# A fused attention, gate and tanh product kernel: fixed steps for each part of a weight conversion, half stores, a third memory for weight pairs, and loads of the last weights one at a time

## The chip, the cores and the metric

The kernel runs on one core of a Trainium2 chip. The metric is the device time of one execution in microseconds (us). The engines are TensorE (PE: matmuls; PEld is its weight load), VectorE (DVE), ScalarE (ACT), GpSimd (POOL) and SyncE (SP). In this kernel every DMA is issued by SP, in the order of the program. Each engine works through its own instructions in order and waits only where an operand or a buffer is not ready.

## The reference

Causal attention with a decay bias gives x (2304 tokens by 512), then a gated product, then a tanh product:

```python
x = attention(q, k, v, s)                                   # 2304 x 512
h1 = 1 / (1 + exp(-(x @ w_gate))) * (x @ w_val)             # 2304 x 1536
y = h1 @ w_out                                              # 2304 x 512
h = y @ w_in                                                # 2304 x 2048
out = (h - tanh(h)) @ w_out2                                # 2304 x 512
```

The weights arrive as 64-bit words and become float32 on the chip.

## The kernel before

**Number format.** Matmuls are done on float32 values split in two: a high part (h), which TensorE's fp32r format holds, and the rest (l). A product is three matmuls: h by h, l by h and h by l. ScalarE makes a high part by a copy; VectorE or GpSimd makes the low part by a subtraction.

**Strassen (Winograd form).** The two products with w_in and w_out2 are done on 2 by 2 blocks with seven products instead of eight. Each operand becomes seven blocks, some of them sums of others. A *weight pair* p (0 to 7) takes rows or columns p and p + 8 of a weight matrix and gives a tile of [128, 2, 7, 256]: high and low parts of seven blocks. *Left* pairs belong to w_in (used in the tanh product), *right* pairs to w_out2 (used in the last product).

**Stages.** Attention and the gate come first (lines 610 to 844) and are not touched. Then:

- *The out-projection loop* (lines 909 to 931): 72 steps, six token blocks of 384 by 12 slices m of 128. A step loads a slice g four steps ahead (`gload`, line 818), splits one two steps ahead into gh (ScalarE, line 826) and gl (VectorE, line 827), with three buffers each and five for g, and issues 12 matmuls (lines 918 to 922). After a block's last slice, `ydrain` takes the four accumulators out, and `ysingle` or `ysums` makes sums (`ydiff`, line 880, VectorE) and splits (`ysplit`, ScalarE line 876, GpSimd line 877), all at once. Beside this, the loop converts the eight right pairs and two left pairs.
- *The tanh product* (lines 963 to 1123): 24 groups (p, j), eight pairs by three double blocks of tokens. A group has seven products of six matmuls (line 991) in the order 1, 6, 7, 2, 5, 4, 3, each drained by ScalarE or VectorE (lines 994 to 1012), then tanh and a subtraction, and two stores of h. Between products `between` runs a step of the six further left conversions, a chore for the last y, or a load of a half right pair.
- *The last product* (lines 1178 to 1196): five token stretches by eight pairs, 40 steps of up to 42 matmuls of 256 columns, and `sprep`, which makes the left operand s from h read back.

**A conversion** (class `PairConversion`, lines 143 to 234) is a list of 14 actions per pair: two scalings of raw words (`words_scale`, ScalarE, line 82), two joins (`words_join`, VectorE, lines 86 and 87), the loads of the next pair, the store of the last pair, four additions (GpSimd, line 184), and high and low parts in two cuts (ScalarE line 199; GpSimd for the first and VectorE for the second, line 204). `tick` runs the next action; the loop calls it so often that the ten conversions end with the 72 steps. Right pairs are made in one tile `stage` and stored to memory (line 855) with a single DMA. Left pairs go to two tiles, `wo0` and `wo1`, in turn. The first two groups of the tanh product write to a tile `temp`, whose tag `wd` holds right pair 0 from the third group on.

Of the kernel before, what the change touches and what calls it, by code (L numbers as in the profile page):

```python
# [67 lines left out]
def attention_moe_moe2(ctx: ExitStack, tc: tile.TileContext, kqT, v, s, wg, wv, wo, win, wo2, out):  # L68
# [15 lines left out]
    def words_join(tmp, raw):  # L84
        lo = raw.bitcast(U).rearrange("p (n two) -> p n two", two=2)[:, :, 0]
        DVE.tensor_scalar(out=tmp, in0=tmp, scalar1=3, scalar2=None, op0=ALU.logical_shift_left)
        DVE.scalar_tensor_tensor(out=tmp, in0=lo, scalar=29, in1=tmp,  # L87
                                 op0=ALU.logical_shift_right, op1=ALU.bitwise_or)

# [53 lines left out]
    class PairConversion:  # L143


        def __init__(self, work, jobs, dst, rest):
            self.raws = [work[:, 0:1024], work[:, 1024:2048]]
            self.u = work[:, 2048:4096].rearrange("p (n c) -> p n c", c=256)
            self.jobs, self.dst, self.rest = jobs, dst, rest
            self.step, self.kept = 0, None  # L150
            self.steps = [f for p in range(len(jobs)) for f in self.pair(p)]
            self.marks = []
            self.load(0)

        def load(self, p):
            if p < len(self.jobs):
                for s in range(2):
                    SP.dma_start(out=self.raws[s], in_=self.jobs[p][1][s])

        def keep(self):  # L160
            if self.kept:
                self.kept()
                self.kept = None

        def pair(self, p):
            kind, _, m = self.jobs[p]
            left = kind == "left"
            t = {"u": self.u, "f": self.u.bitcast(F)}

            def spot(s):  # L170
                return t["u"][:, 2 - 2 * s:4 - 2 * s].rearrange("p a c -> p (a c)")

            def start():
                words_scale(spot(0), self.raws[0])

            def second():
                words_scale(spot(1), self.raws[1])

            def join(s):
                return lambda: words_join(spot(s), self.raws[s])  # L180

            def add(o, x, y, op):
                def f():
                    POOL.tensor_tensor(out=t["f"][:, o], in0=t["f"][:, x], in1=t["f"][:, y], op=op)  # L184
                return f

            if left:
                todo = ((4, 0, 1, ALU.add), (6, 2, 0, ALU.subtract), (5, 4, 2, ALU.subtract), (7, 3, 5, ALU.subtract))
                cuts = ((0, 3, 1), (3, 7, 1))
            else:  # L190
                todo = ((4, 3, 2, ALU.subtract), (6, 1, 3, ALU.subtract), (5, 1, 4, ALU.subtract),
                        (7, 0, 5, ALU.subtract))
                cuts = ((0, 3, 0), (3, 7, 1))

            def high(c0, c1, o):
                def f():
                    if "h" not in t:
                        t["h"], t["l"], t["store"] = self.dst(kind, m)
                    ACT.activation(out=t["h"][:, c0:c1], in_=t["f"][:, c0 + o:c1 + o], func=AF.Copy)
                return f  # L200

            def low(c0, c1, o, last):
                def f():
                    self.rest[last].tensor_tensor(out=t["l"][:, c0:c1], in0=t["f"][:, c0 + o:c1 + o],  # L204
                                            in1=t["h"][:, c0:c1].bitcast(F), op=ALU.subtract)
                    if last:
                        self.kept = t["store"]
                        self.marks.append(p)
                return f

            yield start
            yield second
            yield join(0)
            yield join(1)
            yield lambda: self.load(p + 1)
            yield self.keep
            for a in todo[:2]:
                yield add(*a)
            yield high(*cuts[0])
            for a in todo[2:]:  # L220
                yield add(*a)
            yield low(*cuts[0], False)
            yield high(*cuts[1])
            yield low(*cuts[1], True)
            yield lambda: None

        def tick(self):
            if self.step < len(self.steps):
                self.step += 1
                self.steps[self.step - 1]()  # L230

        def finish(self, p):
            while self.step < len(self.steps) and p not in self.marks:
                self.tick()
# [616 lines left out]
    def dst(kind, p):  # L851
        if kind == "left":
            w = slot[p] = wop.tile([128, 2, 7, 256], R, tag=f"wo{p % 2}", name=f"win{p % 2}")
            return w[:, 0], w[:, 1], None
        return stage[:, 0], stage[:, 1], lambda: SP.dma_start(out=w2scr[p], in_=stage.bitcast(F))

    lefts = [("left", [win[m].bitcast(U).rearrange("p k c -> p (k c)") for m in (p, p + MP)], p) for p in range(MP)]
    rights = [("right", [wo2[m * 128:(m + 1) * 128].bitcast(U) for m in (p, p + MP)], p) for p in range(MP)]
    cvt = PairConversion(work, rights + lefts[:2], dst, (POOL, DVE))
    per = len(cvt.steps) // len(cvt.jobs)  # L860

    ends = [(0, 0), (len(order) - 8, per * MP + 8), (len(order) - 4, per * (MP + 1) + 8),
            (len(order), per * (MP + 2))]

    def ticks(i):
        for (i0, s0), (i1, s1) in zip(ends, ends[1:]):
            if i < i1:
                return s0 + (i + 1 - i0) * (s1 - s0) // (i1 - i0)
# [40 lines left out]
    for i, (blk, m) in enumerate(order):  # L909
# [22 lines left out]
    cvt.finish(len(cvt.jobs) - 1)  # L932
    cvt.keep()
# [4 lines left out]
    cvt = PairConversion(work2, lefts[2:], dst, (POOL, DVE))  # L938
# [3 lines left out]
    temp = wd.tile([128, 3584], F, tag="wd", name="temp")  # L942
    yopen(NJ - 1)
    chores = ysingle(NJ - 1) + ysums(NJ - 1)
# [14 lines left out]

    HT = [fp.tile([128, BLK], F, name=f"ha{k}") for k in range(2)]  # L960
    he = {}

    def group(i, p, j, between):
        w, y = slot[p], Y_[j]
        if i < 2:
            ha, hc = HT
            hb = temp[:, 8 * BLK:9 * BLK]
            o = [temp[:, 2 * BLK * (2 * i + a):2 * BLK * (2 * i + a + 1)].rearrange("p (t c) -> p t c", t=2)
                 for a in range(2)]
        else:  # L970
            if i == 2:
                he["t"] = w2.tile([128, 2, BLK], F, tag="re", name="he")
                WO[0] = wd.tile([128, 2, 7, 256], R, tag="wd", name="wo2f")
                SP.dma_start(out=WO[0].bitcast(F), in_=w2scr[0])
# [9 lines left out]
        for n in PORD:  # L984
# [68 lines left out]
    def sprep():  # L1053
# [7 lines left out]
        if i < 2:  # L1061
            DP["s", i] = wop.tile([128, 2, 7, TB], R, tag=f"wo{i}", name="s")
        sh, sl = (DP["s", i % 2][:, x, :, 0:tb] for x in range(2))
# [3 lines left out]
        POOL.tensor_tensor(out=t[:, 1], in0=t[:, 0], in1=a11, op=ALU.subtract)  # L1067
        ACT.activation(out=sh[:, 0:3], in_=g[:, 1:4], func=AF.Copy)
        DVE.tensor_tensor(out=t[:, 3], in0=a12, in1=t[:, 1], op=ALU.subtract)
        DVE.tensor_tensor(out=sl[:, 0:3], in0=g[:, 1:4], in1=sh[:, 0:3].bitcast(F), op=ALU.subtract)  # L1070
        ACT.activation(out=sh[:, 3:7], in_=t, func=AF.Copy)
        DVE.tensor_tensor(out=sl[:, 3:7], in0=t, in1=sh[:, 3:7].bitcast(F), op=ALU.subtract)
# [3 lines left out]

    loads = []

    def wload(j):
        w = w2.tile([128, 3, 2, 7, 256], R, tag=f"y{j}", name=f"wo2{j}")  # L1080
        for x in range(3):
            WO[1 + 3 * j + x] = w[:, x]
            for q in range(2):
                loads.append((w[:, x, q], w2scr[1 + 3 * j + x][:, q]))

    def wfetch():
        if loads:
            out_, in_ = loads.pop(0)
            SP.dma_start(out=out_.bitcast(F), in_=in_)
# [150 lines left out]
```

## Time and profile before

| | us |
|---|---|
| runs (3), median | 1101.29 |
| lowest and highest | 1099.75, 1102.79 |
| profiled execution | 1103.57 |
| its span, first to last instruction | 1101.8 |

| engine | busy us | share of the span | instructions |
|---|---|---|---|
| PE | 1029.6 | 93% | 7070 |
| PEld | 1007.7 | 91% | 7070 |
| DVE | 728.9 | 66% | 1546 |
| ACT | 536.7 | 49% | 1191 |
| POOL | 539.2 | 49% | 663 |

Successive matmuls overlap in the record, so TensorE's busy share says little of its pace; the distance between starts does. The mean granted TensorE clock is 0.971 of full speed (2.4 GHz). An idle time is named in the rows by what ended it: `<-ACT gh L826` is the gh written by ScalarE on line 826. A wait for several things is put down to the one that came last.

### The profile page before, as it was taken

What the parts mean: (1) busy time and instruction counts of PE and PEld (TensorE: products, weight loads), DVE (VectorE), ACT (ScalarE), POOL (GpSimd) and SP (SyncE); (2) the same over time, 40 slices, a digit from 0 to 9 for tenths busy, and PEclk for the clock granted to TensorE, in tenths of its full rate; (3) what the DMA queues carried; (4) which work ended last, traced back from release to release, by engine and by line L of the source; (5) the groups of instructions that cost most, each with busy time, mean ns of one, the idle gap of its engine ahead of it and who ended that gap; (6) DMA issues with size and microseconds to landing.
All of it is one profiled execution on the core that took longest, in us unless ns stands there. A gap on an engine that the chain in (4) does not pass through costs nothing. (4 is left out here: it accounts for less than half of the span.)

```text
span 1101.8 us, 20467 instructions
## 1 busy us (share of the span) xinstructions
PE 1029.6 (93%) x7070; PEld 1007.7 (91%) x7070; DVE 728.9 (66%) x1546; ACT 536.7 (49%) x1191; POOL 539.2 (49%) x663
## 2 busy tenths in 40 slices
PE   8999999999999999999885867989999989999998
PEld 6899999999999999998785867889999989999998
DVE  7774567776666666374465655577877765888786
ACT  5774656766565665353433333454444433434342
POOL 3575456666565665143325425275555423355342
PEclk9999999999999999999887988899999999999999
DMA  8963457665566563175554575415444299444442
GB/s 214 260 207 107 128 154 195 184 176 169 166 162 173 163 170 94 67 240 178 178 182 144 175 245 184 172 68 220 154 162 153 105 354 358 141 124 139 130 138 74
DMA packets 107455, 187.50 MB, mean 170 GB/s; under 512 B 16276, under 2 KB 76440, under 8 KB 106072
## 3 DMA queue, kind: packets, MB, share of 16 engines
q1 hardware_dynamic: 107352, 186.20, 54.2%
q8 instruction: 55, 0.90, 0.3%
q14 instruction: 48, 0.39, 0.1%
HBM read 133.64 MB, written 52.50 MB: 169 GB/s over the span
## 5 line engine op out<-in xcount | busy, mean ns | idle before, releaser
L918 PE MATMUL bank<-gh,wo 128*128 128x384 f32 x288 | 106.5, 370 | 43.5 <-ACT gh L826 43.5
L991 PE MATMUL bank<-y,win 128*128 128x384 f32 x672 | 120.7, 340 | 4.2 <-ACT ha L994 3.7
L991 PEld LDWEIGHTS bank<-y,win 128*128 128x128 f32 x672 | 118.1, 190 | 5.8 <-ACT ha L994 5.8
L827 DVE TENSOR_TENSOR gl<-g,gh 128x384 fp32r<-128x384 f32 x72 | 58.3, 835 | 97.9 <-ACT gh L826 87.6
L1193 PE MATMUL bank<-wo,s 128*128 128x256 f32 x378 | 106.4, 281 | 2.2 <-DVE s L1070 2.1
L1191 PE MATMUL bank<-wo,s 128*128 128x256 f32 x378 | 105.9, 280 | 0.0
L1192 PE MATMUL bank<-wo,s 128*128 128x256 f32 x378 | 105.9, 280 | 0.0
L919 PE MATMUL bank<-gh,wo 128*128 128x384 f32 x288 | 104.5, 363 | 0.0
L918 PEld LDWEIGHTS bank<-gh,wo 128*128 128x128 f32 x288 | 60.8, 211 | 47.2 <-ACT gh L826 47.2
L500 DVE TENSOR_TENSOR ptl<-bank,pth 128x384 fp32r<-128x384 f32 (+1 forms) x92 | 49.8, 542 | 71.1 <-ACT pth L499 50.5
L499 ACT ACTIVATE pth<-bank 128x384 fp32r<-128x384 f32 (+1 forms) x92 | 44.1, 479 | 107.1 <-PE bank L475 88.8
L958 POOL TENSOR_TENSOR h<-he,h 128x384 f32<-128x384 f32 x44 | 47.5, 1093 | 87.4 <-ACT h L957 87.4
L184 POOL TENSOR_TENSOR work<-work 128x256 f32<-128x256 f32 x64 | 56.8, 898 | 65.6 <-DVE work L87 58.1
L1065 POOL TENSOR_TENSOR dg<-dg 128x256 f32<-128x256 f32 (+1 forms) x40 | 36.6, 915 | 89.3 <-DMA dg<-h 65.1
L604 DVE SCALAR_TENSOR_TENSOR th<-th,bank 128x256 f32<-128x256 f32 (+1 forms) x96 | 42.8, 447 | 47.8 <-PE bank L592 38.2
L1193 PEld LDWEIGHTS bank<-wo,s 128*128 128x128 f32 x378 | 71.2, 188 | 2.9 <-DVE s L1070 2.8
L1191 PEld LDWEIGHTS bank<-wo,s 128*128 128x128 f32 x378 | 71.2, 188 | 0.0
L344 POOL TENSOR_TENSOR kl<-kq,kh 128x576 fp32r<-128x576 f32 (+1 forms) x46 | 56.2, 1221 | 30.7 <-ACT kh L343 29.6
L1192 PEld LDWEIGHTS bank<-wo,s 128*128 128x128 f32 x378 | 71.2, 188 | 0.0
L475 PE MATMUL bank<-ident,sp 128*128 128x128 f32 x400 | 67.7, 274 | 1.6 <-ACT p L487 0.5
L922 PE MATMUL bank<-gl,wo 128*128 128x384 f32 x288 | 67.2, 358 | 0.7 <-DVE gl L827 0.7
L443 ACT ACTIVATE sp<-sp,nm 128x384 f32<-128x384 f32 (+3 forms) x108 | 67.3, 623 | 0.9 <-DVE nm L433 0.8
(381 smaller groups left out, 3395.3 us busy)
## 6 DMA issues: line engine op xcount, KB each, us to landing
h<-h SPq DMA_DIRECT2D x44, 384.0 KB, 3.6
kq<-in_kq SPq DMA_DIRECT2D x32, 448.0 KB, 3.5
w<-stage SPq DMA_DIRECT2D x8, 1792.0 KB, 9.2
g<-g SPq DMA_DIRECT2D x72, 192.0 KB, 5.9
wo<-w SPq DMA_DIRECT2D x12, 896.0 KB, 12.4
dg<-h SPq DMA_DIRECT2D x72, 128.0 KB, 2.3
cbc<-cum SPq DMA_DIRECT2D x32, 256.0 KB, 5.4
work<-in_wo SPq DMA_DIRECT2D x16, 512.0 KB, 3.7
```

The lines of the kernel that those rows point to most:

```text
L184: POOL.tensor_tensor(out=t["f"][:, o], in0=t["f"][:, x], in1=t["f"][:, y], op=op)
L344: POOL.tensor_tensor(out=kl, in0=d["k"], in1=kh.bitcast(F), op=ALU.subtract)
L443: ACT.activation(out=e["sp"], in_=e["sp"], func=AF.Exp, scale=-1.0, bias=e["m"], accum_out=e["sum"])
L475: PE.transpose(e["tr"][j // 4][:, j % 4, :], e["sp"][:, c:c + 128], ident)
L827: DVE.tensor_tensor(out=gl, in0=raw, in1=gh.bitcast(F), op=ALU.subtract)
L918: PE.matmul(acc[d], won[m][0][:, c], gh, start=(m == 0), stop=False)
L919: PE.matmul(acc[d], won[m][1][:, c], gh, start=False, stop=False)
L922: PE.matmul(acc[d], won[m][0][:, c], gl, start=False, stop=(m == M1 - 1))
L991: PE.matmul(ps, l, y[r][:, PR[n], k], start=(k + x == 0 and n != 2), stop=(k == 1 and x == 2), skip_group_check=(n == 2))
L1191: PE.matmul(o, sh[:, g, c], w[:, 0, f], start=(p == 0 and t == 0), stop=False)
L1192: PE.matmul(o, sh[:, g, c], w[:, 1, f], start=False, stop=False)
L1193: PE.matmul(o, sl[:, g, c], w[:, 0, f], start=False, stop=(p == MP - 1 and t == nt - 1))
```

## The change

- `PairConversion` and its `tick` are replaced by `PairWords`, whose parts can be called one by one, and `Plan`, a table from a step's number to the calls to be made in it. `words_join` is cut into a shift and an or.
- In the loop, right pair p has its scalings in step i = 7p + 3, its joins in i + 1 and i + 2, the additions in i + 3 and i + 4, high 0 in i + 4, low 0 in i + 5, high 1 in i + 6, low 1 in i + 7. Its loads are issued in i - 4 and i - 3; its store is two DMAs, high half in i + 8 and low half in i + 9. The two left pairs follow, the second in a work tile of its own.
- The chores of `ysums` and `ysingle` after a block are done one per step.
- Left pairs go to three tiles in turn, `wo0`, `wo1` and `wd`; `temp` serves the first four groups, with `ha` in turn. The conversions and the chores of the last y stand at fixed products in the tanh product. The last tanh and subtraction of a group are put behind the first drain of the next (`hend`).
- Right pairs 0 to 5 are loaded in halves into the y tiles when these come free, one half every 3.5 products; pairs 6 and 7 in halves in the first four steps of the last product. The order of groups is changed (`seq`), and `sprep` for the first two steps is made in six pieces (`sparts`) at fixed products of the last groups.

```diff
-    class PairConversion:
...
+    class PairWords:
...
+        def load(self, s):
+            SP.dma_start(out=self.raws[s], in_=self.jobs[s])
...
+        def high(self, k):
+            c0, c1, o = self.cuts[k]
+            if self.to is None:
+                self.to = self.dst()
+            ACT.activation(out=self.to[:, 0, c0:c1], in_=self.f[:, c0 + o:c1 + o], func=AF.Copy)
+
+        def low(self, k):
+            c0, c1, o = self.cuts[k]
+            (DVE if k else POOL).tensor_tensor(out=self.to[:, 1, c0:c1], in0=self.f[:, c0 + o:c1 + o],
+                                               in1=self.to[:, 0, c0:c1].bitcast(F), op=ALU.subtract)
+
+    class Plan:
+        def __init__(self):
+            self.at = {}
+
+        def put(self, i, f, *args):
+            self.at.setdefault(i, []).append((f, args))
+
+        def do(self, i):
+            for f, args in self.at.pop(i, []):
+                f(*args)
...
+    def left(p, w):
+        def dst():
+            slot[p] = (wd if p % 3 == 2 else wop).tile([128, 2, 7, 256], R, tag=("wo0", "wo1", "wd")[p % 3], name=f"win{p % 3}")
+            return slot[p]
+        return PairWords(w, True, [win[m].bitcast(U).rearrange("p k c -> p (k c)") for m in (p, p + MP)], dst)
+
+    def keep(p, q):
+        SP.dma_start(out=w2scr[p][:, q], in_=stage[:, q].bitcast(F))
...
+    for p in range(MP):
+        c = right(p)
+        i = 7 * p + 3
+        lay(c, {"load0": max(i - 4, 0), "load1": i - 3, "scale0": i, "scale1": i, "shift0": i + 1, "join0": i + 1, "shift1": i + 2, "join1": i + 2,
+                "add0": i + 3, "add1": i + 3, "add2": i + 4, "add3": i + 4, "high0": i + 4, "low0": i + 5,
+                "high1": i + 6, "low1": i + 7})
+        for q in range(2):
+            plan.put(i + 8 + q, keep, p, q)
...
-        while cvt.step < ticks(i):
-            cvt.tick()
+        plan.do(i)
+        if chores:
+            chores.pop(0)()
...
-                for f in (ysums if t else ysingle)(j):
-                    f()
+                chores.extend((ysums if t else ysingle)(j))
...
+    def hend():
+        if "end" in he:
+            he.pop("end")()
...
             if n == 1:
                 ACT.activation(out=ha, in_=ps, func=AF.Copy)
+                hend()
...
-                hfin(o[0][:, 1], ha, DVE)
-                store(0)
-            between()
+                he["end"] = lambda: (hfin(o[0][:, 1], ha, DVE), store(0))
+            plan.do(len(PORD) * i + len(P) - 1)
...
-    seq = [(0, 0), (0, 1), (1, 0), (0, 2), (1, 1), (1, 2)]
-    seq += [(p, j) for p in range(2, MP - 2) for j in range(NJ)]
-    seq += [(p, j) for j in range(NJ) for p in (MP - 2, MP - 1)]
+    seq = [(0, 0), (0, 1), (1, 0), (1, 1), (0, 2), (1, 2)]
+    seq += [(p, j) for p in range(2, MP - 3) for j in range(NJ)]
+    seq += [(p, j) for j in range(NJ) for p in range(MP - 3, MP)]
...
+    for k, f in zip((1, 2, 3, 5, 7, 8, 9, 10, 14, 15, 16), ysingle(NJ - 1) + ysums(NJ - 1)):
+        plan.put(k, f)
+    for p in range(2, MP):
+        k = n * (2 * p - 1 + (p == MP - 1))
+        h = (k + 13, k + 17) if p == 2 else (k + 7, k + 14)
...
+    for j in range(2):
+        k = n * (seq.index((MP - 1, j)) + 1)
+        plan.put(k, wload, j)
+        for x in range(6):
+            plan.put(k + 7 * x // 2, wfetch)
...
+    k = n * seq.index((MP - 1, NJ - 1))
+    for x, i in enumerate((k - 13, k - 11, k - 7, k - 6, k - 5, k - 3)):
+        plan.put(i, next, parts[0], None)
+        plan.put(i + n, next, parts[1], None)
...
     for i, (s, p) in enumerate(dsteps):
+        if loads:
+            wfetch()
```

## Rows read from the trace of the kernel before

**Rows 1.** Busy time by stage: stretch, length, busy (instructions) by engine, granted clock, DMA.

```profile
505.05:721.28 216.23, 172.03 (x867) 168.01 (x865) 113.98 (x141) 77.75 (x135) 83.50 (x64) 0.87 0.53 181
721.28:914.85 193.57, 181.77 (x1010) 178.89 (x1009) 143.77 (x231) 82.09 (x154) 97.93 (x86) 0.97 0.51 186
914.85:1096.90 182.05, 179.89 (x1513) 179.02 (x1512) 143.13 (x191) 69.32 (x85) 76.92 (x79) 1.00 0.49 149
```

**Rows 2.** TensorE's timeline at the loop's start: start, length, instruction.

```profile
505.05 0.33 PE L918 MATMUL bank<-gh,wo 128*128 128x384 f32 x1
...
507.13 0.33 PE L918 MATMUL bank<-gh,wo 128*128 128x384 f32 x1
```

**Rows 3.** Busy time of two stretches: the tanh product's end, and the last product.

```profile
900.00:915.00 15.00, 9.91 (x42) 9.59 (x41) 10.18 (x16) 5.19 (x9) 4.75 (x5) 0.77 1.02 420
950.00:1000.00 50.00, 50.00 (x426) 50.00 (x425) 42.20 (x54) 18.20 (x21) 23.80 (x21) 1.00 0.47 135
```

**Rows 4.** TensorE's waits in the loop: us in total, times, longest.

```profile
PE bank L918 <- ACT gh L826: 43.5, 11, 5.9
```

**Rows 5.** ScalarE's waits in the loop.

```profile
ACT stage L199 <- DMA w<-stage: 57.9, 6, 13.2
...
ACT gh L826 <- DMA g<-g: 15.1, 4, 6.3
```

**Rows 6.** Busy time of three stretches behind a wait of TensorE.

```profile
544.11:550.00 5.89, 5.89 (x22) 5.89 (x23) 3.20 (x2) 1.61 (x3) 5.81 (x5) 0.61 0.24 67
735.77:742.83 7.06, 7.06 (x32) 7.06 (x32) 4.75 (x8) 4.94 (x9) 7.06 (x5) 0.76 0.30 114
907.75:914.16 6.41, 6.41 (x21) 6.41 (x22) 3.67 (x7) 1.01 (x2) 0.51 (x1) 0.52 1.01 416
```

**Rows 7.** TensorE's waits after the loop; then its costliest group there.

```profile
PE bank L991 <- ACT ha L994: 11.2, 4, 5.1
PE bank L1193 <- DVE s L1070: 2.1, 2, 1.6
...
L991 PE MATMUL bank<-y,win 128*128 128x384 f32 x672 | 120.7, 340 | 4.2 <-ACT ha L994 3.7
```

**Rows 8.** DMA issues of the whole span: count, KB each, median us to landing.

```profile
h<-h SPq DMA_DIRECT2D x44, 384.0 KB, 3.6
...
w<-stage SPq DMA_DIRECT2D x8, 1792.0 KB, 9.2
g<-g SPq DMA_DIRECT2D x72, 192.0 KB, 5.9
```

**Rows 9.** Timeline of VectorE and GpSimd after the second block.

```profile
576.39 1.83 POOL L877 TENSOR_TENSOR y<-ra,y 128x768 fp32r<-128x768 f32 x1 [8.21 <-ACT y L876]
576.42 2.62 DVE L880 TENSOR_TENSOR re<-rd,ra 128x768 f32<-128x768 f32 x1
...
578.18 2.52 POOL L877 TENSOR_TENSOR y<-rc,y 128x768 fp32r<-128x768 f32 x1
```

**Rows 10.** Single lines in the loop: least, median and longest ns of one.

```profile
L827 DVE TENSOR_TENSOR gl<-g,gh x71: 543/559/2181, 504.7 to 717.2; 128x384 fp32r<-128x384 f32 x71
...
L204 POOL TENSOR_TENSOR stage<-work,stage x8: 1822/1830/1846, 520.3 to 689.3; 128x768 fp32r<-128x768 f32 x8
L204 DVE TENSOR_TENSOR stage<-work,stage x8: 1210/1212/2874, 525.0 to 692.4; 128x1024 fp32r<-128x1024 f32 x8
...
L184 POOL TENSOR_TENSOR work<-work x40: 727/936/1105, 516.0 to 718.7; 128x256 f32<-128x256 f32 x40
...
L880 DVE TENSOR_TENSOR ra<-rc,ra x2: 948/948/949, 574.5 to 654.9; 128x768 f32<-128x768 f32 x2
...
L87 DVE SCALAR_TENSOR_TENSOR work<-work x20: 691/693/1214, 515.0 to 714.8; 128x512 uint32<-128x512 uint32 x20
...
L86 DVE TENSOR_SCALAR work<-work x20: 410/420/2040, 514.5 to 714.3; 128x512 uint32<-128x512 uint32 x20
```

**Rows 11.** SP's waits in the loop.

```profile
SPq L158 <- DVE work L87: 65.7, 18, 15.4
```

More of the change, by code (lines that the diff above doesn't have):

```diff
@@ L141, in finish, with __init__ @@
                 self.tick()
-    class PairConversion:
-        def __init__(self, work, jobs, dst, rest):
+    class PairWords:
+        def __init__(self, work, left, jobs, dst):
             self.raws = [work[:, 0:1024], work[:, 1024:2048]]
             self.u = work[:, 2048:4096].rearrange("p (n c) -> p n c", c=256)
[L149 to L185, printed above, removed]
@@ L187, in pair @@
+            self.f = self.u.bitcast(F)
+            self.jobs, self.dst, self.to = jobs, dst, None
             if left:
[L188 to L193 removed]
@@ L195, in high @@
[L195 to L230, printed above, removed]
@@ L232, in finish @@
-        def finish(self, p):
-            while self.step < len(self.steps) and p not in self.marks:
-                self.tick()
+                self.todo = ((4, 0, 1, ALU.add), (6, 2, 0, ALU.subtract), (5, 4, 2, ALU.subtract),
+                             (7, 3, 5, ALU.subtract))
+                self.cuts = ((0, 3, 1), (3, 7, 1))
+            else:
+                self.todo = ((4, 3, 2, ALU.subtract), (6, 1, 3, ALU.subtract), (5, 1, 4, ALU.subtract),
+                             (7, 0, 5, ALU.subtract))
+                self.cuts = ((0, 3, 0), (3, 7, 1))
@@ new lines, in load, with spot, scale, shift @@
+        def load(self, s):
+            SP.dma_start(out=self.raws[s], in_=self.jobs[s])
+        def spot(self, s):
+            return self.u[:, 2 - 2 * s:4 - 2 * s].rearrange("p a c -> p (a c)")
+        def scale(self, s):
+            words_scale(self.spot(s), self.raws[s])
+        def shift(self, s):
+            words_shift(self.spot(s))
+        def join(self, s):
+            words_or(self.spot(s), self.raws[s])
+        def add(self, k):
+            o, x, y, op = self.todo[k]
+            POOL.tensor_tensor(out=self.f[:, o], in0=self.f[:, x], in1=self.f[:, y], op=op)
@@ L849, in attention_moe_moe2 @@
     Y_, slot, raws = {}, {}, {}
[L851 to L868, printed above, removed]
+    def right(p):
+        return PairWords(work, False, [wo2[m * 128:(m + 1) * 128].bitcast(U) for m in (p, p + MP)], lambda: stage)
@@ new lines, in left, with lay @@
+    def left(p, w):
[5 more added lines that the diff above has]
+        SP.dma_start(out=w2scr[p][:, q], in_=stage[:, q].bitcast(F))
+    plan = Plan()
+    rest = {}
+    def lay(c, at):
+        for what, i in at.items():
+            plan.put(i, getattr(c, what[:-1]), int(what[-1]))
@@ L870, in yraw, with second @@
+    def second():
+        c = left(1, w2.tile([128, 4096], U, tag=f"y{NJ - 1}l", name="workb"))
+        lay(c, {"load0": 64, "load1": 64, "scale0": 67, "scale1": 67, "shift0": 68, "join0": 68, "shift1": 69, "join1": 69, "add0": 70,
+                "add1": 70, "add2": 71, "add3": 71, "high0": 70, "low0": 71, "high1": 72, "low1": 72})
+    plan.put(63, second)
+    chores = []
     def yraw(k):
@@ L941, in attention_moe_moe2 @@
     WO = {}
-    temp = wd.tile([128, 3584], F, tag="wd", name="temp")
+    temp = wd.tile([128, 10 * BLK], F, tag="wd", name="temp")
     yopen(NJ - 1)
-    chores = ysingle(NJ - 1) + ysums(NJ - 1)
     DP = {}
@@ L958, in hfin, with group @@
         eng.tensor_tensor(out=o, in0=x, in1=o, op=ALU.subtract)
+    def hend():
+        if "end" in he:
+            he.pop("end")()
     HT = [fp.tile([128, BLK], F, name=f"ha{k}") for k in range(2)]
     he = {}
-    def group(i, p, j, between):
+    def group(i, p, j):
         w, y = slot[p], Y_[j]
[L965 to L968, printed above, removed]
+        if i < 4:
+            ha = HT[i % 2]
+            hb, hc = (temp[:, x * BLK:(x + 1) * BLK] for x in (8, 9))
+            o = [temp[:, 2 * BLK * (2 * (i % 2) + a):2 * BLK * (2 * (i % 2) + a + 1)].rearrange("p (t c) -> p t c", t=2)
                  for a in range(2)]
         else:
-            if i == 2:
+            if i == 4:
                 he["t"] = w2.tile([128, 2, BLK], F, tag="re", name="he")
-                WO[0] = wd.tile([128, 2, 7, 256], R, tag="wd", name="wo2f")
-                SP.dma_start(out=WO[0].bitcast(F), in_=w2scr[0])
             ha = HT[i % 2]
@@ L1075, in sprep, with wtile @@
         S_["s", i] = sh, sl
+    def sprep():
+        for _ in sparts():
+            pass
     loads = []
+    def wtile(w, p):
+        WO[p] = w
+        loads.extend((w[:, q], w2scr[p][:, q]) for q in range(2))
     def wload(j):
@@ L1081, in wload @@
         for x in range(3):
[L1082 to L1084 removed]
+            wtile(w[:, x], 3 * j + x)
     def wfetch():
[L1087 to L1093 removed]
@@ L1094, in attention_moe_moe2 @@
-    free = {p: max(i for i, (q, j) in enumerate(seq) if q == p) for p in range(MP)}
-    need = {p: min(i for i, (q, j) in enumerate(seq) if q == p) for p in range(MP)}
-    def between():
-        i, n = S_["group"]
-        if chores:
-            chores.pop(0)()
-            return
-        p = 2 + cvt.step // per
-        if p < MP:
-            for _ in range(2 if i == need[p] - 1 else 1):
-                if cvt.step < len(cvt.steps) and (cvt.step % per < 8 or i > free[p - 2]):
-                    cvt.tick()
-        S_["group"][1] += 1
-        if n % 2 == 0:
-            wfetch()
@@ L1111, in attention_moe_moe2 @@
-    for i, (p, j) in enumerate(seq):
-        S_["group"] = [i, 0]
-        group(i, p, j, between)
-        p = 2 + cvt.step // per
-        if p < MP and i == need[p] - 1:
-            cvt.finish(p - 2)
-        if (MP - 1, j) == seq[i]:
-            if j == 0:
-                d_open()
-            if j < NJ - 1:
-                wload(j)
-        if seq[i] == (MP - 2, NJ - 1):
-            sprep()
-    while loads:
-        wfetch()
-    sprep()
+        out_, in_ = loads.pop(0)
+        SP.dma_start(out=out_.bitcast(F), in_=in_)
@@ L1129, in attention_moe_moe2 @@
+    assert not plan.at
+    wtile(wop.tile([128, 2, 7, 256], R, tag="wo1", name="wo2e"), MP - 2)
+    wtile(w2.tile([128, 2, 7, 256], R, tag=f"y{NJ - 1}h", name="wo2l"), MP - 1)
+    hend()
     dsteps = [(s, p) for s in range(NSB) for p in range(MP)]
     acc = {}
-    WO[MP - 1] = w2.tile([128, 2, 7, 256], R, tag=f"y{NJ - 1}h", name="wo2l")
-    SP.dma_start(out=WO[MP - 1].bitcast(F), in_=w2scr[MP - 1])
     ot = w2.tile([128, 10, 512], F, tag=f"y{NJ - 1}l", name="o")
```

40 lines of the change are left out of this document (30 added, 10 removed).

## The prediction

> **What bounds the kernel now.** First the busy time by stage [rows 1]: the three stages that the diff touches are the out-projection loop (505.05 to 721.28 us, "the loop"), the tanh product (to 914.85) and the last product (to the end). TensorE runs in all of them; the question is how far each is from TensorE's own pace. The pace comes from the timeline: the first matmul of two successive steps of the loop starts at 505.05 and 507.13 [rows 2], so a step of 12 matmuls of 384 columns takes 2.08 us, 0.1733 each. The loop has 72 steps: 149.8 us, against 216.2 measured. The tanh product has 24 groups of 42 such matmuls, 1008 x 0.1733 = 174.7, against 193.6. The last product has 1512 matmuls of 256 columns at 50.00/426 = 0.1174 us [rows 3], 177.5, against 182.05 up to its last matmul at 1096.9 (the trace's first and last starts; 4.9 us of drain follow and stay). So 66.4, 18.9 and about 4 us are lost in the three stages.
>
> Then the waits. In the loop TensorE waits 43.5 us, all for gh, the high half of the activation [rows 4]. ScalarE makes gh, and ScalarE stands 57.9 us in six waits for the store of the converted weight pair [rows 5]: it may not write the first three columns of the next pair into the one stage tile before the store of the last has landed. The longest is 13.2 us; the gh behind each comes late and TensorE stands. The store, 1,835,008 bytes, is issued behind two 512 KB loads, and three ticks (one or two steps) before the write that needs it. That the wait also costs clock is seen where it ended: after it, from 544.11 to 550, 22 matmuls took 5.89 us at a granted clock of 0.61, half-way to the 1.2 GHz level, instead of 3.8 [rows 6], 2.1 us lost; eleven waits at about 2 us are the 22 us that 43.5 leaves of the 66.4.
>
> In the tanh product four waits make 11.2 us [rows 7]: 3.7 at its start, 5.1 at its end, and 2.4 in two within. Behind the first and the last the clock is low again: 32 matmuls in 7.06 us and 21 in 6.41 [rows 6], 1.5 and 2.8 us more than at pace. That is 15.5 of the 18.9.
>
> **The change, part by part.**
>
> *Stage store and fixed steps in the loop.* A store is now two halves of 917,504 bytes, issued one and two steps into the next pair's seven-step round; the first write that needs half 0 is in step 4 and the one that needs half 1 in step 5. That is three steps, 6.2 us, and the SP queue runs ahead of that by some steps; half of what lands in 9.2 us [rows 8] needs less. So the 57.9 us go, and with them the 43.5 and the clock. What is late next?
>
> *The queue.* SP has two loads and two stores per round, in four successive steps, each with a 196,608-byte g load. SP issues g for step i+4 as soon as the split of step i-1 is done, and each of the four stops waits for work one step later than that. So g keeps about four steps, 8.3 us, against 5.9 us to landing [rows 8]. At the 420 GB/s of a full stretch [rows 3] the heaviest steps carry 1.11 MB, 2.65 us in 2.08, twice, then 0.72 MB, 1.7 us: a backlog of 1.1 us that drains. I take nothing; the bound above is the third rival.
>
> *VectorE and GpSimd.* This is what I expect to be late next. The timeline at 576 us shows them take turns [rows 9]: ydiff starts at 576.42, while GpSimd's ysplit (576.39, 1.83 us) runs, and takes 2.62 us where it takes 0.95 alone; the next ysplit, at 578.18, is stretched to 2.52. 0.95 plus the rest of the other's time is what is seen: one stands while the other works. So their times add up. By the least or median time of each [rows 10], for the whole loop: GpSimd 40 adds x 0.73 = 29.2, 10 low halves x 1.82 = 18.2, 14 ysplits x 1.82 = 25.5; VectorE 72 gl x 0.56 = 40.3, 20 joins x (0.42 + 0.69) = 22.2, 10 low halves x 1.21 = 12.1, 8 ydiff x 0.95 = 7.6. Sum 155.1 us, above TensorE's 149.8. In the old loop this fitted into 216.
>
> The Trainium skill, "SBUF — State Buffer", section "Who interferes with whom", says the same as a rule: a VectorE instruction with two SBUF inputs and a GpSimd instruction that reads SBUF contend, and the later one blocks fully. By it alone the loop can't be under 155; without it 150 would be the floor. The trace agrees (2.62 against 0.95).
>
> Spread over the loop: a plain seven-step round asks 4.74 us of GpSimd, 3.4 of VectorE's conversion and 3.9 of gl, 12.1 in 14.6 us of TensorE. That is covered. After a second token block the nine chores of ysums stand in nine successive steps: 5 x 1.82 + 4 x 0.95 = 12.9, with gl 5.0 and 9/7 of a round's conversion 10.5, together 28.4 us in 18.7. That is 9.7 too much. Cover: the drain of the block ends VectorE's lead, so gl stands two steps ahead, 4.2 us, less some 1.1 for gh and gl; 3.1 us. 6.6 us fall on TensorE, and about 1.9 of clock (between the 1.5 and the 2.8 above). Two such stretches (after the second and the fourth block): 17.0 us. After the other blocks there are two chores, 7.1 us in 4.2, which the 3.1 cover. Loop: 149.8 + 17.0 = 166.8. Bounds: 149.8 (nothing lost, or both engines let their own less urgent work wait) and 207 (third rival). Gain 49.4.
>
> *First loads at step 0 and scale at step 3* instead of at once: this is inside these numbers; the early wait goes with the others.
>
> *Tanh product.* The last tanh and subtraction of a group now come after the copy of the next group's first bank, and the first groups use both ha tiles in turn where two groups shared one: the two waits within go, 2.4 us, and most of 3.7 + 1.5 at the start. The same 11 chores remain there, now over 16 steps of 1.04 us, so I leave 2.7 of the 5.2. The third memory and the fixed steps take the conversions off the ends of groups; pair 2 is ready three steps, 3.1 us, ahead of use, and its first write waits for a store from temp, six steps after that is issued, against 3.6 us to landing [rows 8]. Nothing; were it late, up to 3.6 once. At the end the 12 half loads came in groups 20 to 23; now they are 12 in groups 18 to 23, one per 3.5 steps, and four are moved into the last product. 917,504 bytes per 3.64 us are 252 GB/s, and the stores of h 2 x 393,216 per 7.28 us 108: 360, under the 420 of a full stretch [rows 3]. So the stores land and ScalarE isn't held, and the first s is made in pieces in the two groups before: 5.1 + 2.8 go. What is left is the unexplained 3.4 and the 2.7: 174.7 + 6.1 = 180.8, gain 12.8; bounds 5 (loads still bunch at the end) and 17.
>
> *Last product.* s for both first steps is ready; TensorE's 2.1 us of waits for s [rows 7] go. The four late half loads are issued one per step of 42 x 0.1174 = 4.9 us, for use from step 6. Gain 2, bounds 0 and 4.
>
> **Sum.** 49.4 + 12.8 + 2.0 = 64.2. The profiled execution took 1103.57, its span 1101.8; 1103.57 - 64.2 = 1039.4. The median of the runs is 2.28 lower, so 1037.
>
> **Rivals.** (1) *TensorE is the bound throughout.* The chores' overload is hidden: ysplits can lag, since the y tiles are needed only a stage later. Against it: ScalarE's and GpSimd's orders are fixed, and the adds queue behind the ysplits. Loop 151, tanh product 177.5, last 179: gain 65 + 16 + 3 = 84, 1017. (2) *GpSimd lags in every round:* its adds reach 0.94 at the median [rows 10], ScalarE waits for them at the second high half, as it did, and gh stands behind. Two us in each of ten rounds: loop 187, 1057. (3) *The burst of four transfers makes g late:* 2.5 us and 2 of clock in each of nine rounds, 40 us: loop 207, 1077. For it: 15.1 us of ScalarE's waits are for g already [rows 5]; against: those stand behind the old bunch of 2.9 MB. (4) *The halves don't part:* if the first write must wait for both halves, a step is gone; about 3 us in 8 rounds: 1061. (5) *Slower: SP's stops decide.* SP stood 65.7 us for the joins [rows 11]; there are now four stops per round, 36 in all, where there were some 18. If each costs TensorE a step and the clock, 2.08 + 1.9, the loop is 150 + 143 = 293, and the time 1163. It decides from (66.4 + 14.8)/36 = 2.3 us per stop. Against it: each stop lies after work that is one step off, not three.
>
> **Chances.** Forecast 0.52; (1) 0.15; (2) 0.16; (3) 0.08; (4) 0.04; (5) 0.05. The range 1014 to 1065 takes the forecast with its bounds, (2), (4) and (1); it leaves out (3), (5) and the outer ends of (1) and (2). A difference of 0.3% is about what a measurement of this kernel tells from none. Only (5) is slower; (3) in a worse form could end within 0.3%.
>
> **What would show it.** ScalarE's wait for the store gone from the loop; the loop 165 to 170 us, its idle in the two stretches after the second and fourth block, released by gl; VectorE plus GpSimd busy over 150 in it; granted clock 1.00 elsewhere. In the tanh product no wait over 2 us behind the first group, and none at its end. I am wrong if the idle is spread over every round (2), is released by g (3), or if ScalarE still waits for the stage.

## The result and the profile after

The changed kernel takes 1026.12 us (median of 4 runs, 1025.32 to 1029.07) against 1100.52 (4 runs): a ratio of 0.9327, 95% interval 0.9301 to 0.9353, so 74.4 us less. Forecast were 1037 and 64.2 us. The busy time by stage, as in [rows 1] (stretch, length, busy and instructions of PE, PEld, DVE, ACT, POOL, then granted clock, DMA share, GB/s):

```profile
503.20:659.50 156.30, 152.38 (x866) 151.03 (x865) 120.41 (x141) 77.74 (x134) 88.00 (x64) 0.99 0.73 250
659.50:838.90 179.40, 176.28 (x1011) 175.00 (x1009) 138.71 (x234) 83.81 (x156) 97.61 (x88) 1.00 0.56 197
838.90:1018.85 179.95, 179.64 (x1513) 179.10 (x1512) 140.49 (x189) 68.03 (x84) 78.52 (x78) 1.00 0.49 154
```

The loop went from 216.2 to 156.3 us, the tanh product from 193.6 to 179.4, the last product from 182.05 to 179.95. Of the 78.3 us between the two spans, 1.9 lie ahead of the loop, where nothing was changed; this start lay between 503.0 and 505.5 in all profiles here. The granted clock of the loop rose from 0.87 to 0.99. All that TensorE still waits for from 500 us to the end is this (us in total, times, longest; L916 and L912 are the loop's matmuls, L985 the tanh product's):

```profile
PE bank L916 <- DVE gl L800: 2.5, 1, 2.5
PE bank L985 <- ACT ha L988: 2.3, 3, 1.6
PE bank L912 <- ACT gh L799: 1.2, 1, 1.2
PE bank L985 <- DVE win L193: 0.8, 1, 0.8
PE bank L1192 <- DVE s L1067: 0.3, 1, 0.3
```

The 43.5 us of [rows 4] are 1.2. ScalarE's waits in the loop, to be read against [rows 5]: the store of the stage isn't among them, and the longest is 4.0 us.

```profile
ACT gh L799 <- PE bank L913: 34.5, 32, 1.6
ACT gh L799 <- DMA g<-g: 8.3, 6, 4.0
...
ACT work L82 <- POOL stage L193: 5.2, 3, 2.4
ACT stage L189 <- POOL work L183: 5.1, 3, 2.8
```

The first row is the healthy one: ScalarE is ahead and waits for a gh buffer that TensorE still reads. The DMA issues (count, KB each, us to landing) answer [rows 8]:

```profile
w<-stage SPq DMA_DIRECT2D x16, 896.0 KB, 4.3
g<-g SPq DMA_DIRECT2D x72, 192.0 KB, 4.4
```

### The profile page after: what moved, and what is told of

Its sections match the earlier page's. It is cut to its first block, busy times and chain, and to the rows that moved or that the text cites. A ratio compares the mean times of both kernels' runs of the same rounds, so it can differ in the third digit from the quotient of the medians.

```text
span 1023.5 us, 20474 instructions
## 1 busy us (share of the span) xinstructions
PE 1003.2 (98%) x7070; PEld 986.5 (96%) x7070; DVE 727.9 (71%) x1546; ACT 537.6 (53%) x1191; POOL 545.9 (53%) x663
## 5 line engine op out<-in xcount | busy, mean ns | idle before, releaser
L985 PE MATMUL bank<-y,win 128*128 128x384 f32 x672 | 118.5, 337 | 2.8 <-ACT ha L988 2.0
L985 PEld LDWEIGHTS bank<-y,win 128*128 128x128 f32 x672 | 116.8, 188 | 3.8 <-ACT ha L988 2.6
L912 PE MATMUL bank<-gh,wo 128*128 128x384 f32 x288 | 96.9, 336 | 1.2 <-ACT gh L799 1.2
L913 PE MATMUL bank<-gh,wo 128*128 128x384 f32 x288 | 96.6, 336 | 0.0
L800 DVE TENSOR_TENSOR gl<-g,gh 128x384 fp32r<-128x384 f32 x72 | 64.5, 907 | 35.2 <-ACT gh L799 21.4
L950 POOL TENSOR_TENSOR h<-he,h 128x384 f32<-128x384 f32 x40 | 43.2, 1099 | 69.9 <-ACT h L949 69.9
L183 POOL TENSOR_TENSOR work<-work 128x256 f32<-128x256 f32 x60 | 53.6, 906 | 45.4 <-DVE work L89 44.6
L317 POOL TENSOR_TENSOR kl<-kq,kh 128x576 fp32r<-128x576 f32 (+1 forms) x46 | 56.2, 1222 | 30.5 <-ACT kh L316 29.6
L1065 ACT ACTIVATE s<-dg 128x768 fp32r<-128x768 f32 (+1 forms) x40 | 31.3, 781 | 75.5 <-PE bank L1191 67.2
L799 ACT ACTIVATE gh<-g 128x384 fp32r<-128x384 f32 x72 | 37.0, 523 | 53.8 <-PE bank L913 34.5
```

What stands on the lines that cost most here:

```text
L183: POOL.tensor_tensor(out=self.f[:, o], in0=self.f[:, x], in1=self.f[:, y], op=op)
L317: POOL.tensor_tensor(out=kl, in0=d["k"], in1=kh.bitcast(F), op=ALU.subtract)
L800: DVE.tensor_tensor(out=gl, in0=raw, in1=gh.bitcast(F), op=ALU.subtract)
L912: PE.matmul(acc[d], won[m][0][:, c], gh, start=(m == 0), stop=False)
L913: PE.matmul(acc[d], won[m][1][:, c], gh, start=False, stop=False)
L985: PE.matmul(ps, l, y[r][:, PR[n], k], start=(k + x == 0 and n != 2), stop=(k == 1 and x == 2), skip_group_check=(n == 2))
```

## The experiments

Twelve kernels were run. "Loop" is the time from its first matmul to the first of the tanh product. Ratios are to the kernel before. A difference from the changed kernel is taken between medians; the kernel before, timed beside each set of runs, had medians from 1100.5 to 1102.2, so such a difference is good to about 2 us. The loop is read from one profile each; in the three kernels below whose loop is that of the changed kernel (156.3) it took 156.1 to 156.4.

**What held ScalarE: the length of the store, or its place.** First the halves alone, at the old place.

```diff
-        return stage[:, 0], stage[:, 1], lambda: SP.dma_start(out=w2scr[p], in_=stage.bitcast(F))
+        return stage[:, 0], stage[:, 1], lambda: [SP.dma_start(out=w2scr[p][:, q], in_=stage[:, q].bitcast(F)) for q in range(2)]
```

> The kernel before with one edit: the stage store is issued as two halves (high, then low) at the same place in the list of actions. Theory 1 (the place of the store in the round decides, its length less): the first write of the next pair needs only the high half, which lands some 3 us sooner than the whole; ScalarE's wait for the store falls from 57.9 to about 35 us, the loop from 216 to about 198, the time to about 1082. Rival (halving alone is the gain): the wait falls under 10 us and the loop comes to about 165, the time to about 1048. Rival (the lump of chores and the stops of SP are the loss): no change, 1098 to 1101.

1092.87 us, ratio 0.9915 (0.9894 to 0.9936); loop 205.3. ScalarE's wait for the store is still

```profile
ACT stage L199 <- DMA w<-stage: 47.6, 6, 12.0
```

so halving gains 11 us of the loop's 60. My own estimate of the gain, 18 us, was too large: at this place, behind the two loads, a half still takes 7.4 us to land, against 4.3 in the changed kernel.

Then the place alone: the whole store as the last action of its own pair.

```diff
             yield lambda: self.load(p + 1)
-            yield self.keep
+            yield lambda: None
...
             yield low(*cuts[1], True)
-            yield lambda: None
+            yield self.keep
```

> The kernel before with one edit: the whole store is issued as the last action of its pair, directly behind its last write, eight actions (some four steps) earlier. Theory 1 (the place decides): ScalarE no longer waits for the store (57.9 us to under 15), but SP now stands for the low half in the same step, so g comes late by up to 3 us per round; the loop 180 to 190, the time 1065 to 1075. Rival (halving alone is the gain): ScalarE still waits some 4 us per round, no gain above 10 us. Rival (SP's stops decide): slower than 1101.

1076.05 us, ratio 0.9754 (0.9737 to 0.977); loop 188.6. ScalarE no longer waits for the store at all. It now waits for g, because SP stands at the store until the low half is there (two rows of ScalarE's waits, then one of SP's):

```profile
ACT gh L826 <- DMA g<-g: 62.3, 14, 8.0
...
ACT stage L199 <- POOL work L184: 8.2, 2, 4.3
```

```profile
SPq L855 <- DVE stage L204: 56.2, 8, 10.5
```

The whole store also lands in 6.8 us at this place, where it took 9.2 behind the loads. This is what the fixed steps are for: a DMA is issued so many steps behind the work that it waits for that SP stands less. In the changed kernel the same wait of SP for the low half (`L834 <- DVE stage L193`) makes 23.0 us in eight, that for the high half 10.0 in seven, and g comes in time.

The other way round, the changed kernel with a whole store:

```diff
-        for q in range(2):
-            plan.put(i + 8 + q, keep, p, q)
+        plan.put(i + 9, keep, p, slice(0, 2))
```

> The changed kernel with one edit undone: the right pair is stored whole, in step i + 9, instead of in halves in i + 8 and i + 9. Theory 1 (the place decides): the first write of the next pair stands in i + 11; SP issues the store about one step after the last write, and 9 us to landing against two to three steps (4 to 6 us) leaves ScalarE up to 3 us per round to wait, of which two steps of lead cover most: loop 156 to 162, the time 1026 to 1032. Rival (halving is the gain): waits of 5 us and more in each of eight rounds reach TensorE, loop over 180, the time over 1050.

1028.11 us, ratio 0.9329 (0.9311 to 0.9346), the same as the changed kernel within the intervals; loop 158.3, 2.0 longer. ScalarE waits for the store again, but the lead covers most of it (TensorE's waits for gl grow from 2.5 to 5.0 us):

```profile
ACT stage L189 <- DMA w<-stage: 17.6, 6, 5.2
```

**The chores in a lump.**

```diff
                 chores.extend((ysums if t else ysingle)(j))
+                while chores:
+                    chores.pop(0)()
```

> The changed kernel with one edit undone: the chores after a block are done all at once at the block's end, as before. Theory 1: ScalarE and VectorE are held by the chain of differences and splits (about 8 us by the trace of before, with two steps, 4.2 us, of lead): 4 us and the clock, 2 us, at each of two blocks, about 1 at the other two: loop 168, the time 1038. Rival (the lump was the loss in the old loop): loop over 190, the time over 1060. Rival (the two engines only take turns, whatever the order): same as the changed kernel within 3 us.

1036.30 us, ratio 0.9394 (0.938 to 0.9408); loop 165.0, with 11.2 us of wait for gh in two places, one for each ysums. So the loop's way is 216.2, 188.6 with the store in another place, 165.0 with fixed steps and halves, 156.3 with one chore per step. (These versions are not nested edit by edit; the steps between them are differences of whole versions, and the fixed steps were not undone alone.)

**Do VectorE and GpSimd take turns, and does that set the loop?** Theory 1 is the one of the prediction: their times add up, to 155.1 us. The test takes away the fourteen subtractions by which GpSimd reads SBUF for y, or doubles them.

```diff
-        POOL.tensor_tensor(out=yl, in0=raws[k], in1=yh.bitcast(F), op=ALU.subtract)
+        if j < NJ - 1:
+            POOL.memset(yl.bitcast(F), 0.0)
+        else:
+            POOL.tensor_tensor(out=yl, in0=raws[k], in1=yh.bitcast(F), op=ALU.subtract)
```

> The changed kernel, but for the first two y tiles GpSimd fills the low part of y with zero instead of subtracting: its fourteen instructions read no SBUF, and the output lacks that low part. Theory 1 (VectorE with two inputs and GpSimd take turns, and the stretch behind the second block is where the loop still loses): the longest gl falls from 2.2 to under 1.3 us, TensorE's wait of 2.5 us for gl goes, the loop comes from 156.3 to 151 to 153, the time to about 1022. Rival (what is left comes from DMA or from ScalarE): the loop stays within 1 us of 156.3.

1019.29 us, ratio 0.9252 (0.9237 to 0.9268). The loop's row:

```profile
503.80:653.60 149.80, 149.80 (x867) 149.80 (x866) 97.35 (x141) 77.66 (x134) 63.53 (x64) 1.00 0.77 261
```

149.8 us is TensorE's pace to the tenth, with no wait and no lost clock, better than the 151 to 153 expected. One point missed: the longest gl is still 2.2 us, as GpSimd's low half of a weight pair, 1.82 us, still runs once per round.

```diff
-        POOL.tensor_tensor(out=yl, in0=raws[k], in1=yh.bitcast(F), op=ALU.subtract)
+        for _ in range(2 if j < NJ - 1 else 1):
+            POOL.tensor_tensor(out=yl, in0=raws[k], in1=yh.bitcast(F), op=ALU.subtract)
```

> The changed kernel, but GpSimd makes the low part of the first two y tiles twice, fourteen more instructions of 1.82 us, 25.5 us more. Theory 1 (the times of the two engines add up, 155.1 us before, 180.6 now, against 149.8 of TensorE): the loop cannot be under 175, the time about 1045 to 1050. Rival (GpSimd was busy 88 of 156 us and has room): the loop grows by under 8 us, the time stays under 1035.

1048.65 us, ratio 0.9519 (0.9505 to 0.9533). The loop's row, and TensorE's longest waits in it:

```profile
503.60:682.20 178.60, 158.23 (x865) 153.47 (x865) 139.57 (x141) 77.45 (x134) 117.36 (x78) 0.97 0.65 219
```

```profile
PE bank L917 <- DVE gl L800: 14.5, 10, 3.9
PE bank L913 <- ACT gh L799: 5.9, 3, 4.4
```

25.5 us more on GpSimd made the loop 22.3 us longer, though GpSimd had been busy only 88 of 156 us. Room by its own busy time it had; room beside VectorE it had not. The sum was 180.6, the loop 178.6. The plainest sign is VectorE's own busy time: the same 141 instructions took 97.4 us with GpSimd's reads for y away, 120.4 in the changed kernel and 139.6 with them doubled.

The sum itself is a rough measure. Laid over each other, the two timelines leave 16 of the 156.3 us of the changed kernel's loop, and 17 of the 178.6, in which neither engine runs, so the sums of least times are somewhat too large for a floor; and the 178.6 hold 20.4 us of waits and some 8 of clock and short gaps, which the sum does not know. That sum and loop lie within 2 us of each other is in part chance.

**Does the place of the chores matter beside the sum?**

```diff
-        if chores:
+        if chores and (i - 3) % 7 != 1:
             chores.pop(0)()
```

> The changed kernel, but no chore is done in the step of a round's first join; the chores after a block then end a step or two later. Theory 1 (the sum of the two engines' times decides, and no work is taken away): the loop 155 to 157 as it is, the time within 2 us of the changed kernel. Rival (where the chores lie in the round decides, as the prediction's stretch had it): the stretch behind the second block loses 2 to 4 us less, loop 153, the time 1022 to 1024.

1023.99 us, ratio 0.9296 (0.9283 to 0.9309); loop 153.9. The time alone is not parted from the changed kernel's by the intervals, but the loop is, by far more than the 0.3 us among equal loops. Theory 1 missed here and the rival came near: no work was taken away, and the loop lost 2.4 us and lies 1.2 under the sum. The place has a share, and the sum by least durations is no floor to the microsecond: a low half of the second left pair (1.2 us) falls behind the loop's end, and two gl (1.1) ahead of its start.

**A version that beats both.** VectorE does one of these subtractions in 0.95 us, where GpSimd takes 1.82.

```diff
-        POOL.tensor_tensor(out=yl, in0=raws[k], in1=yh.bitcast(F), op=ALU.subtract)
+        (DVE if j < NJ - 1 else POOL).tensor_tensor(out=yl, in0=raws[k], in1=yh.bitcast(F), op=ALU.subtract)
```

> The changed kernel, but the low part of the first two y tiles is subtracted by VectorE instead of GpSimd. Theory 1 (the loop takes the greater of two sums: TensorE's 149.8 us, and VectorE's and GpSimd's added up): fourteen times 1.82 - 0.95 = 12.2 us leave the second sum, 155.1 to 142.9, so TensorE's 149.8 is left and some for the stretches, where VectorE has 18 us of its own in 18.7: loop 150 to 153, the time 1020 to 1023. Rival (each engine's own load counts: VectorE goes from 120 busy to over 130 of 156 us and its order is strict): the loop grows to over 158, the time over 1028.

1019.32 us, ratio 0.9254 (0.9241 to 0.9267), 6.8 under the changed kernel by the medians. The loop:

```profile
504.30:654.10 149.80, 149.80 (x867) 149.80 (x866) 114.80 (x155) 77.76 (x134) 58.06 (x50) 1.00 0.76 261
```

VectorE has fourteen more instructions (155 for 141) and is busy 5.6 us *less* than in the changed kernel: the fourteen take 17.4 us, and its other instructions became 23.0 us shorter in all. The same for the last y, in the tanh product (the condition on j left out):

> The same, and also the low part of the last y tile, made at the start of the tanh product, on VectorE. Theory 1 (there too the engines take turns, but VectorE drains the banks as well and was busy 24 of the first 29 us before): the start of the tanh product changes by -1 to +2 us, the time 1019 to 1024. Rival (VectorE's order holds the banks): waits for ha at the start, +3 to +6 us over the version with the first two tiles alone.

1019.76 us, ratio 0.9266 (0.9249 to 0.9283): no difference, as theory 1 had it.

**The tanh product's three edits.** The end of a group as before:

```diff
-                he["end"] = lambda: (hfin(o[0][:, 1], ha, DVE), store(0))
+                hfin(o[0][:, 1], ha, DVE)
+                store(0)
```

> The changed kernel with one edit undone: the last tanh and subtraction of a group stand in their own group again, ahead of the next group's copy of its first bank. Theory 1 (ScalarE stands for the sum before it may copy the first bank, about 1 us per place, mostly covered by eight banks; the old waits of 1.3 and 1.1 us had a conversion's high and low part beside it): TensorE loses 0 to 2.5 us, the time 1026 to 1029. Rival (the order at a group's end was the tanh product's loss): over 5 us, the time over 1031.

1027.90 us, ratio 0.9333 (0.9318 to 0.9347); tanh product 181.8, 2.4 us more in the profile, and the median 1.8 more, which the intervals don't part from nothing. (The kernel with the chores in a lump, whose tanh product is the changed kernel's, took 181.6 for it in its profile, so a gain of this edit is not shown.)

The loads of the last weights behind each other:

```diff
-            plan.put(k + 7 * x // 2, wfetch)
+            plan.put(k + x, wfetch)
```

> The changed kernel, but the six half loads of the last weights behind each y tile are issued behind six successive products instead of every 3.5. Theory 1 (the end wait of the old tanh product came from both the bunch and s made in one piece): the stores of h land later, ScalarE stands for them up to 5 us, but the eight banks cover that: TensorE loses 0 to 2 us, the time 1026 to 1029. Rival (the bunch was the cause): 5 us of wait and 3 of clock come back, 1034.

1034.77 us, ratio 0.9392 (0.9378 to 0.9406). The rival's time, at another place: the wait, 4.5 us for a bank that VectorE had yet to drain, stands at the first matmuls of the last product. ScalarE's row just ahead of it shows why (start, length, instruction, idle before and what ended it), and the stretch behind it the clock:

```profile
844.09 0.49 ACT L949 ACTIVATE h<-bank 128x384 f32<-128x384 f32 x1 [5.51 <-DMA h<-h]
```

```profile
840.00:850.00 10.00, 5.52 (x30) 5.32 (x29) 4.80 (x8) 2.00 (x4) 3.03 (x3) 0.73 0.69 259
```

A tile of h was still being stored, behind five loads that SP issued between 823.8 and 827.2 us: one store took 14.0 us to land, where the median of the run is 2.9. The drain behind it came too late for the next matmuls. My theory that eight banks cover such a wait was wrong at this place.

s in one piece:

```diff
-    for x, i in enumerate((k - 13, k - 11, k - 7, k - 6, k - 5, k - 3)):
-        plan.put(i, next, parts[0], None)
-        plan.put(i + n, next, parts[1], None)
+    for x in range(6):
+        plan.put(k - 1, next, parts[0], None)
+        plan.put(k + n - 1, next, parts[1], None)
```

> The changed kernel, but s for each of the first two steps of the last product is made in one piece, behind the last but one and the last group, instead of in six pieces within them. Theory 1 (s in one piece stands ahead of the next group's copy of the first bank, on ScalarE, behind a chain of VectorE and GpSimd): a wait of 3 to 5 us for ha at the last group and up to 3 us of clock, the time 1031 to 1034. Rival (the bunch of loads was the cause): same as the changed kernel within 2 us.

1030.08 us, ratio 0.935 (0.9336 to 0.9364): 4.0 more than the changed kernel, between the two expectations, though the intervals meet. TensorE's waits for ha grow from 2.3 to 4.6 us, the longest 2.2, and those for s from 0.3 to 1.2, with no fall of the clock. So of the two edits at the old end the spread loads are worth about 8.6 by the medians, s in pieces 3 to 4. Each was undone alone in the changed kernel, where the order of the groups is new too; that the old wait of 5.1 with its clock had both causes is likely, but neither was tried in the kernel before.

## Why the prediction was right, and where its size was off

*ScalarE's wait for the store.* Right: 57.9 us gone, and with it nearly all of the 43.5 and the clock. The cause that the prediction gives, the store's length and its three ticks, holds by its second half: the place gives 27.6 us of the loop alone, though new waits for g are in it, the halves 11 alone, and in the finished plan 2.0, which the intervals don't part from nothing. "Half lands in less" was not what counted.

*The queue.* Right at no cost: g lands in 4.4 us. The early store gives an idea of the third and fifth rivals: with SP standing 56.2 us for the low half, ScalarE waits 62.3 us for g, and the loop takes 188.6.

*VectorE and GpSimd.* Right in kind: they take turns, and the loop is TensorE's 149.8 where the sum is the smaller (129.6, with the zero fills counted at nothing, and 142.9) and longer where it is the greater (156.3 for 155.1, 178.6 for 180.6). With the same 155.1 it also took 153.9 and 165.0, as the chores lie, so the sum does not give the length alone. The Trainium skill's rule ("SBUF — State Buffer", section "Who interferes with whom") is borne out in this loop: gl goes from 0.56 to 2.15 us beside GpSimd's subtractions. The prediction's floor of 155 "by it alone" counts the twenty shifts too (8.4 us), which have one SBUF input where the rule, as it is told there, speaks of two; without them the sum is 146.7, under TensorE's 149.8. The trace says that they belong in it: a shift of 0.42 us that starts during a ysplit takes 2.06 and ends just behind it.

```profile
621.05 2.00 POOL L871 TENSOR_TENSOR y<-re,y 128x768 fp32r<-128x768 f32 x1
621.27 2.06 DVE L85 TENSOR_SCALAR work<-work 128x512 uint32<-128x512 uint32 x1
```

**The term that was mis-sized is "Two such stretches: 17.0 us".** It measured 6.5 for the whole loop. I took all 28.4 us of a stretch as due in its nine steps, and added the excess to TensorE's time, once per stretch. The timeline of GpSimd behind the second block shows what happens instead:

```profile
562.92 3.42 POOL L183 TENSOR_TENSOR work<-work 128x256 f32<-128x256 f32 x3 [1.09 <-DVE work L89]
566.31 2.16 POOL L871 TENSOR_TENSOR y<-rc,y 128x768 fp32r<-128x768 f32 x1
568.43 2.55 POOL L193 TENSOR_TENSOR stage<-work,stage 128x768 fp32r<-128x768 f32 x1
570.94 2.18 POOL L871 TENSOR_TENSOR y<-re,y 128x768 fp32r<-128x768 f32 x1
573.07 2.16 POOL L871 TENSOR_TENSOR y<-rb,y 128x768 fp32r<-128x768 f32 x1
575.19 2.79 POOL L871 TENSOR_TENSOR y<-rd,y 128x768 fp32r<-128x768 f32 x1
```

GpSimd runs without a gap from 562.92 to 577.98, each instruction stretched as in [rows 9]. The last ysplit belongs to step 32, which TensorE leaves at about 572 (503.2 + 33 x 2.08); it is done 6 us later, and nobody waits for it. So the stretch had some twelve steps, not nine. Beside it VectorE:

```profile
569.21 4.32 DVE L800 TENSOR_TENSOR gl<-g,gh 128x384 fp32r<-128x384 f32 x2
573.45 2.87 DVE L193 TENSOR_TENSOR stage<-work,stage 128x1024 fp32r<-128x1024 f32 x1
576.24 2.15 DVE L800 TENSOR_TENSOR gl<-g,gh 128x384 fp32r<-128x384 f32 x1
```

Here a gl takes 2.15 us where it needs 0.56, until its lead is used up: TensorE's one wait for gl, 2.5 us, ends behind the last of these rows. VectorE has no gap from 569.21 on, so what held TensorE was VectorE's stretched instructions and not a wait of VectorE for GpSimd's results. This is the only place in the loop where the granted clock fell; the last two rows are the first matmuls with gl of two successive steps:

```profile
565.00:575.00 10.00, 9.90 (x57) 9.51 (x56) 10.00 (x6) 6.68 (x11) 9.92 (x6) 1.00 0.61 222
575.00:585.00 10.00, 7.50 (x35) 7.18 (x34) 9.78 (x12) 3.95 (x8) 7.28 (x7) 0.83 0.76 234
```

```profile
578.44 1.65 PE L916 MATMUL bank<-gl,wo 128*128 128x384 f32 x4 [2.50 <-DVE gl L800]
...
582.05 0.88 PE L916 MATMUL bank<-gl,wo 128*128 128x384 f32 x4
```

This step took 3.61 us instead of 2.08: 1.5 us by clock. Behind the fourth block, where the round stands at another phase, the chores lag too and TensorE has no wait at first. The lag reaches it later, behind the fifth block: the last ysplit runs until 634.0, GpSimd's low half of a weight pair comes behind it, ScalarE stands 2.4 us for that half ahead of the drain (the longest in its row `ACT work L82 <- POOL stage L193` above), and gh is 1.2 us late at 638.6.

```profile
632.18 1.85 POOL L871 TENSOR_TENSOR y<-rd,y 128x768 fp32r<-128x768 f32 x1
633.98 2.15 POOL L193 TENSOR_TENSOR stage<-work,stage 128x768 fp32r<-128x768 f32 x1
```

These make 5.2 of the 6.5 us; the rest are gaps under half a microsecond. That ysplits can lag I had given to the first rival, with 0.15, and argued down ("the adds queue behind the ysplits"); they do queue, and it cost little. The two steps of lead I had counted (3.1 us per stretch); not counted was that the last ysplits may end some three steps late, and that the sum overstates what the two engines need. The result lies between the forecast and that rival's 1017.

*The tanh product.* 180.8 forecast, 179.4 measured; most of the waits named are gone (11.2 to 3.1 us, 1.6 of it at the start). Of the 14.2 us some 8 lie in the last 15 us of the stage, the 5.1 of wait and 2.8 of clock that the prediction named, 3.5 in the first 60 us and the rest between. The order at a group's end could give about 2 of these six; the third memory, the fixed products and the new order of groups were not undone alone, so their shares stay open.

*The last product.* 2.0 forecast, 2.1 measured: the waits for s went from 2.1 to 0.3.

## What to carry to other kernels

Where a tile is stored and written again, give the store a place in the order that is some steps behind the last write and some steps ahead of the next; the length of the transfer then matters little. Add up the times of VectorE's instructions that read SBUF and of GpSimd's that do, and set the sum against TensorE's time, as a warning and not as a floor: an engine that is busy half the time may have no room left, and moving work to the faster of the two can free both. An overload of a few steps costs only what the lead and the work that nobody yet waits for don't cover, so ask of each piece who waits for it before adding it to the bound.

## What the runs showed of the hardware

I had not expected how much taking turns makes of an engine's busy time: 25.5 us more on GpSimd made the loop 22.3 longer and VectorE's same instructions 19.2 us longer, and fourteen instructions more on VectorE left it busy 5.6 us less. A blocked instruction shows as a longer one, not as idle time, and a shift with one SBUF input is blocked like a subtraction with two (0.42 to 2.06 us). A DMA share of 0.96 to 1.02 from 800 to 850 us, across the change from the tanh product to the last (326 to 391 GB/s), cost TensorE no wait, where the loads issued in a row cost 4.5 us and the clock.
